# Wide conversion pieces, deferred transposing reads and the place of the value products in a top-k attention and MLP kernel

## The chip, the cores and the metric

The kernel runs on one core of one Trainium2 chip. The time is that of one execution on the device in microseconds (us), and a kernel is judged by the median of its runs. All inputs and the output lie in HBM.

## What is computed

An attention block that keeps the 32 largest scores of a row, and a two-layer MLP with a smooth activation:

```python
batch, n_heads, seq, head_dim = (8, 8, 576, 64)
scores = scale * np.matmul(q, k.transpose(0, 1, 3, 2))
kth = np.partition(scores, -top_k, axis=-1)[..., -top_k:-top_k + 1]
scores = np.where(scores >= kth, scores, -1000000000.0)
scores = scores - np.max(scores, axis=-1, keepdims=True)
attn = np.exp(scores)
attn = attn / (np.sum(attn, axis=-1, keepdims=True) + 1e-09)
x = np.matmul(attn, v)            # heads side by side: 4608 rows of 512
h = x @ w_in                      # 512 -> 2048
g = np.where(h >= 1, h, np.where(h <= -1, 0.0, (h + 1) ** 2 / 4))
out = g @ w_out                   # 2048 -> 512
```

`q`, `k` and `v` are float32. The two weight matrices are float64, so that the kernel reads 8 bytes per weight (16.8 MB in all) and makes float32 values of them itself.

## The kernel before

**Steps.** The unit of work is a step: 128 query rows of two heads against all 576 keys. There are 144 of them, 18 for each batch entry. Four steps with the same rows (all eight heads) make a chunk of 128 rows of `x`, and there are 36 chunks. The step runs over the engines like this:

- TensorE (PE) makes the scores `sp` (L351); ScalarE (ACT) copies them to `s` (L352).
- VectorE (DVE) finds the 32nd largest score of each row: pairwise maxima and minima `more` and `less` (L365), lists of eight (`max`, L413 to L439) with `match_replace` between them (L372), a scan that merges the lists (L444), and the masking of the exponentials `e` (L451). ACT makes `e` (L388).
- The weights of the step, `e` divided by its sum, have to be transposed. In the first steps PE does this by matmuls with a diagonal matrix `diag` (L401, L466) and ACT copies the result to `wT` (L469). In all later steps `move_w` does it: ACT splits `e` into 16-bit halves (`halves`, L481; one buffer), SP's queue writes them to HBM (`rows`, L483) and reads them back transposed (`wT`, L484; four buffers).
- `values` multiplies `wT` with the values (`po`, L498; L506 for the steps with the last rows of two batch entries), and ACT copies `po` to `xT` (L511). `po` uses the three PSUM buffers of the tag `ph`.

**The MLP.** When a chunk is complete, `mlp` puts its 32 pieces of work into the list `pending`: eight `hidden` (16 TensorE instructions `ph`, L531, with ACT's `r` and `g`, L535 and L542, and three of GpSimd (POOL), L547 to L549) and sixteen `final` (2 instructions `py`, L554, of 512 columns). `advance` takes them from the list between the parts of the steps, in amounts that a small model of the time in the kernel decides (`due`, `pe_time`, `usable`). One unit of `cost` is one 128-column product or a quarter of a `final`; a chunk has 128 units.

**The conversion of the weights.** In the first steps ("early") the float64 words are converted as well. A piece has 128 x 256 weights: its words are loaded by SP into one of eight slots of `room` (L132; the slots lie in the space of the second `kT` and `v_in`, and carry these names in the profile), ACT makes `units` from the low words and the sign of the high words (L145, L146), DVE shifts the high words (`bits`, L154), and POOL adds the two into `w_in` or `w_out` (L156). There are 64 pieces. Four are converted ahead of the first step, seven in each of the steps 0 to 7, four in step 8. Later, `inspect_piece` (L171) reads all weights a second time, 256 words at a time, to see that none is too small for the method.

**Keys, queries and values.** From the third batch entry on, `turn` transposes keys and queries as `move_w` does weights: ACT makes `parts` (L276), SP writes `lines` (L278) and reads them back transposed (L279). `turned_keys_of` does a fifth of a batch entry's keys in every second step, and issues the loads of the values (`v_in` L193, `v_tail` L196 and L200) in the last three of these parts.

**The order.** The instructions of PE, DVE, ACT and POOL stand in the order in which the program issues them (`manual_schedule`). The order of SP, which issues all DMAs, is made by the framework's scheduler. All of them are queues: an instruction that waits holds up those behind it.

Of the kernel before, what the change touches and what calls it, by code (L numbers as in the profile page):

```python
# [11 lines left out]
F32 = mybir.dt.float32  # L12
# [14 lines left out]
def kernel(  # L27
# [14 lines left out]
    P = 128  # L42
# [62 lines left out]

    WC = 256
    n_pieces = NK * DFF // WC + NF * DM // WC
    n_steps = B * (NT * NHP + NHP // 2)
    excess = const.tile([P, 2 * n_steps + n_pieces], F32, name="excess")
    signs = const.tile([P, 2, n_pieces], F32, name="signs")  # L110

# [13 lines left out]

    def load(pool, i, bufs=3):
        if i < n_pieces and i not in loaded:
            if room:
                loaded[i] = room[i % 8]
            else:  # L130
                loaded[i] = pool.tile([P, 2 * WC], U32, name="raw", bufs=bufs)
            nc.sync.dma_start(out=loaded[i], in_=pieces_of_weights[i][1].bitcast(U32))  # L132

    def words_of(pool, i, bufs=3):
        load(pool, i, bufs)
        words = loaded.pop(i).rearrange("p (n t) -> p n t", t=2)
        return words[:, :, 0], words[:, :, 1]

    def convert_piece(pool, i, any_size):

        lo, hi = words_of(pool, i)
        dst = pieces_of_weights[i][0]
        units = pool.tile([P, WC], F32, name="units", bufs=3)
        if not any_size:
            nc.scalar.activation(units, lo, AF.Identity, bias=one, scale=2.0 ** -52)  # L145
            nc.scalar.activation(units.bitcast(BF16).rearrange("p (n t) -> p n t", t=2)[:, :, 1], hi.bitcast(F32), AF.Sign)  # L146
        else:
            nc.scalar.activation(units, lo, AF.Identity, bias=two, scale=2.0 ** -51)
            sign = pool.tile([P, WC], F32, name="sign", bufs=3)
            nc.scalar.activation(sign, hi.bitcast(F32), AF.Sign)  # L150
        yield

        bits = pool.tile([P, WC], U32, name="bits", bufs=3)
        nc.vector.tensor_scalar(bits, hi, 3, None, ALU.logical_shift_left)  # L154
        if not any_size:
            nc.gpsimd.tensor_tensor(out=dst.bitcast(I32), in0=bits.bitcast(I32), in1=units.bitcast(I32), op=ALU.add)  # L156
        else:
            nc.gpsimd.tensor_tensor(out=bits.bitcast(I32), in0=bits.bitcast(I32), in1=units.bitcast(I32), op=ALU.add)
            size = pool.tile([P, WC], F32, name="units", bufs=3)
            nc.scalar.activation(size, hi.bitcast(F32), AF.Abs)  # L160
            nc.vector.scalar_tensor_tensor(out=sign, in0=size, scalar=TINY, in1=sign, op0=ALU.is_ge, op1=ALU.mult)

            nc.vector.tensor_scalar(bits.bitcast(F32), bits.bitcast(F32), LARGEST, -LARGEST, ALU.min, ALU.max)
            nc.gpsimd.tensor_tensor(out=dst, in0=sign, in1=bits.bitcast(F32), op=ALU.mult)
        yield

    def inspect_piece(pool, i):

        lo, hi = words_of(pool, i, 1)
        for x in range(2):  # L170
            nc.scalar.activation(lo.bitcast(F32), hi.bitcast(F32), AF.Sign, bias=tiny[:, x:x + 1],  # L171
                                 accum_out=signs[:, x, i:i + 1])


    def run(ctx, paired):
# [12 lines left out]
        def load_values(b):  # L188
            v_in = stage.tile([P, H, NT, D], F32, name="v_in")
            v_tl = v_tails[b % 2]  # L190
            yield v_in, v_tl
            for h in range(0, H, 2):
                nc.sync.dma_start(out=v_in[:, h:h + 2], in_=whole(v, b)[:, h:h + 2])  # L193
                yield
            for j in range(2):
                nc.sync.dma_start(out=v_tl[0][j * TL:(j + 1) * TL, j::2, :],  # L196
                                  in_=v[b, j::2, SM:S, :].rearrange("h p d -> p h d"))
            for hp in range(NHP):
                g = hp % 2
                nc.sync.dma_start(out=v_tl[1][g * TL:(g + 1) * TL, 2 * hp:2 * hp + 2, :],  # L200
                                  in_=v[b, 2 * hp:2 * hp + 2, SM:S, :].rearrange("h p d -> p h d"))
            yield

# [68 lines left out]
        def turn(x, dst):  # L272

            n = x.shape[0]
            parts = stage.tile([P, 2, H * D], U16, name="parts", tag="k_tl", bufs=1)[0:n]
            nc.scalar.copy(parts, x.rearrange("p h d -> p (h d)").bitcast(U16).rearrange("p (k t) -> p t k", t=2))  # L276
            lines = dram.tile([P, 2, H * D], U16, name="lines")[0:n]
            nc.sync.dma_start(out=lines, in_=parts)  # L278
            nc.sync.dma_start_transpose(dst.bitcast(U16), lines.rearrange("p t k -> (p t) k"))  # L279

        def turned_keys_of(b):
# [14 lines left out]

            blocks = {0: load_block(0)}
            yield got
            for c in range(NT + 1):
# [3 lines left out]
                turn(blocks.pop(c)[0:n], kT[:, :, c * P:c * P + n])  # L303
                if c == 1:
                    loads = load_values(b)
                    got["v"], got["v_tl"] = next(loads)
                if 1 <= c < NT:
                    next(loads)
                elif c == NT:
                    for _ in loads:  # L310
                        pass
                yield got
# [164 lines left out]
        def move_w(st):  # L477
# [4 lines left out]
            rows = dram.tile([P, 2, 2 * S], U16, name="rows")  # L482
            nc.sync.dma_start(out=rows, in_=halves)  # L483
            nc.sync.dma_start_transpose(wT.bitcast(U16), rows.rearrange("p t k -> (p t) k"))  # L484

# [116 lines left out]
        def convert(time):  # L602
# [8 lines left out]
            usable[converted] = time  # L611
            for i in range(begun, converted + (7 if room else 3)):
                load(words, i)

        def inspect():
            nonlocal inspected
            if paired and inspected < n_pieces:
                inspect_piece(late, inspected)
                inspected += 1


        K_TIME, PIECE_TIME, UNIT_TIME, SLOTS, EARLY_SHARE = 10.1, 0.55, 0.218, 7, 48
        pe_time, dve_time, done, scored, ready_at, usable = 9.0, 12.0, {}, {}, {}, {0: 0.0}

        def advance(amount, until):

            nonlocal spent, due, pe_time
            due = due + amount if pending else 0.0
            pe_time = max(pe_time, until - 4.0)
            while pending:  # L630
                cost, pieces, work, _ = pending[0]
                if pieces > converted or usable[pieces] > pe_time + 0.5:
                    break
                if due < cost or pe_time >= until:
                    break
                pending.popleft()
                due -= cost
                spent += cost
                pe_time += cost * UNIT_TIME
                work()  # L640
            due = min(due, 24.0)
# [12 lines left out]
        if paired:  # L654
            for x in (stage.tile([P, NHP, S], F32, name="kT").rearrange("p h n -> p (h n)"),
                      stage.tile([P, H, NT, D], F32, name="v_in").rearrange("p h c d -> p (h c d)")):
                room.extend(x[:, c:c + 2 * WC].bitcast(U32) for c in range(0, 8 * WC, 2 * WC))

# [6 lines left out]
        fetch(0)  # L665
        prep = None
        state = []
# [29 lines left out]
        next(first)  # L697
        for i in range(2, 8 if room else 3):
            load(words, i)
# [3 lines left out]
        begin_at(0)  # L703
        for i in range(3):
            convert(13.0)
        for _ in first_top(state[0]):
# [20 lines left out]
        for m in range(n + 2):  # L727
# [14 lines left out]
            if m < n:  # L742
                top_k = weights(state[m], state[m - 1] if m > 0 else None, state[m + 1] if m + 1 < n else None)
                parts = [1] * SLOTS if early else [1, 1, 0, 1, 1, 1, 1]
                start = max(dve_time, scored[m])
                now_converting = range(SLOTS)
                dve_time = start + K_TIME + PIECE_TIME * min(len(now_converting), n_pieces - converted)
                done[m] = dve_time
                state[m]["by_tensor"] = early or m >= n - 2
            for slot in range(SLOTS):  # L750
# [6 lines left out]
                elif slot == 3 and late is not None:  # L757
                    if m % 2:
                        inspect()
                    elif paired:  # L760
                        load(late, inspected, 1)
                if slot == 1 and 1 <= m <= n and state[m - 1]["by_tensor"]:
# [12 lines left out]
                if slot == 2 and not early:  # L775
                    values_until((m - 2) // 2 * 2)
                if slot == (4 if early else 2):
                    begin_at(m + 2)
                if slot == (6 if early else 1):
# [4 lines left out]
                    if prep is not None and (m % 2 == 0 or next_keys == 1):  # L784
# [59 lines left out]
```

## Time and profile before

| | |
|---|---|
| median of 3 runs | 1515.24 us (1515.05 to 1516.16) |
| profiled execution | 1516.81 us, span 1514.6 us, mean granted clock 0.98 |
| PE, DVE, ACT, POOL busy | 1441.9, 1412.7, 1167.1, 921.8 us |
| DMA | 259.76 MB, mean 172 GB/s |
| `units`, `bits`, add (L145, L146, L154, L156) | 64 instructions each |

In the profile, a row of a group reads: line, engine, operation, what is written from what, shapes, count | busy time, mean of one | idle time before, and what ended it. In a timeline a row begins with the start in us from the begin of the span and the duration in us; `[1.75 <-PE pw L466]` at its end means that the engine was idle for 1.75 us before it, until a `pw` of PE. PEld is the loading of weights on TensorE, PEclk the granted share of TensorE's clock, SPq the issue of a DMA by SP. A matmul in float32 appears as two instructions.

### The profile page before, as it was taken

How to read it: one execution, taken by the hardware profiler on the slowest of the kernel's cores; microseconds unless marked ns; L12 is line 12 of the kernel's file. 1: busy time of each engine (PE TensorE's matmuls, PEld its weight loads, DVE VectorE, ACT ScalarE, POOL GpSimd, SP SyncE). 2: the span in 40 equal slices, each digit the busy share in tenths (PEclk: the TensorE clock that was granted, in tenths of full speed). 3: DMA queues.
4: the chain of work that ended last, by engine and by line, in shares of the span. 5: the costliest groups of instructions: out<-in, count | busy, mean ns of one | idle time of the engine just before them, and what ended most of it. 6: DMA issues, size and time to landing. Idle time of an engine off the chain costs nothing.

```text
span 1514.6 us, 32180 instructions
## 1 busy us (share of the span) xinstructions
PE 1441.9 (95%) x10625; PEld 1042.8 (69%) x10625; DVE 1412.7 (93%) x4424; ACT 1167.1 (77%) x2288; POOL 921.8 (61%) x1339
## 2 busy tenths in 40 slices
PE   5588999999999999999999999899999999999998
PEld 4466677777777777677777777666677777777675
DVE  7888999999999999999999999999999999999912
ACT  7896878787778888787778888677777887777732
POOL 4563666666666666566666666566666666666630
PEclk7798999999999999999999999999999999999999
DMA  9542567775687777886677877786677777656510
GB/s 258 159 136 61 147 173 177 194 199 160 166 190 202 197 195 187 206 205 171 167 199 199 201 185 189 183 215 172 162 198 179 208 181 179 160 157 153 143 29 17
DMA packets 512448, 259.76 MB, mean 172 GB/s; under 512 B 459152, under 2 KB 467344, under 8 KB 512272
## 3 DMA queue, kind: packets, MB, share of 16 engines
q1 hardware_dynamic: 512272, 257.62, 65.6%
q8 instruction: 86, 1.41, 0.4%
q14 instruction: 90, 0.74, 0.2%
HBM read 62.91 MB, written 102.04 MB: 109 GB/s over the span
## 4 chain that ended last, share of the span: by engine, by line
PE 85%; ACT 8%; DMA 2%; issue 2%; POOL 1%; DVE 0%; SPq 0%; ACTq 0%; POOLq 0%; DVEq 0%
PE py L554 32%; PE ph L531 30%; PE sp L351 10%; PE po L498 10%; PE pw L466 2%; ACT halves L481 1%; ACT e L388 1%; ACT units L145 1%; PE po L506 1%; DMA rows<-halves 1%; ACT s L352 1%; DMA wT<-rows 1%; ACT wT L469 1%; ACT raw L171 0%; ACT g L542 0%
## 5 line engine op out<-in xcount | busy, mean ns | idle before, releaser
L531 PEld LDWEIGHTS ph<-xT,w_in 128*128 128x128 f32 x4608 | 547.0, 192 | 101.7 <-issue 82.2
L531 PE MATMUL ph<-xT,w_in 128*128 128x128 f32 x4608 | 557.2, 276 | 3.2 <-POOL w_in L156 3.1
L554 PE MATMUL py<-w_out,g 128*128 128x512 f32 x1152 | 551.0, 603 | 0.0
L547 POOL TENSOR_SCALAR r<-r 128x256 f32<-128x256 f32 x276 | 161.5, 585 | 447.2 <-ACT r L535 447.1
L372 DVE MATCH_REPLACE8 more<-tops,more 128x288 f32<-128x288 f32 x864 | 375.1, 437 | 0.0
L554 PEld LDWEIGHTS py<-w_out,g 128*128 128x128 f32 x1152 | 198.1, 191 | 181.2 <-issue 165.3
L481 ACT COPY halves<-e 128x1152 uint16<-128x1152 uint16 x266 | 291.9, 1143 | 15.5 <-DMA rows<-halves 14.5
L451 DVE SCALAR_TENSOR_TENSOR e<-s,kth,e 128x577 f32<-128x577 f32 x288 | 251.8, 909 | 3.6 <-ACT e L388 3.5
L549 POOL TENSOR_TENSOR g<-r,g 128x256 f32<-128x256 f32 x280 | 227.8, 814 | 22.0
L535 ACT ACTIVATE r<-ph,half 128x256 f32<-128x256 f32 (+1 forms) x296 | 136.1, 460 | 130.3 <-PE ph L531 104.2
L388 ACT ACTIVATE e<-s,nmax 128x576 f32<-128x576 f32 x288 | 222.4, 773 | 4.7
L404 POOL TENSOR_SCALAR e<-e,rz 128x576 f32<-128x576 f32 x266 | 223.4, 850 | 0.0
L352 ACT ACTIVATE s<-sp 128x576 f32<-128x576 f32 x288 | 172.0, 650 | 52.4 <-PE sp L351 51.9
L548 POOL TENSOR_TENSOR r<-r 128x256 f32<-128x256 f32 x276 | 191.3, 693 | 23.0
L351 PE MATMUL sp<-kT,qT 64*128 64x288 f32 x1024 | 162.9, 434 | 10.9 <-ACT kT L254 9.5
L498 PE MATMUL po<-wT,v_in 128*64 128x128 f32 x2048 | 143.4, 281 | 17.3 <-ACT g L542 15.3
L498 PEld LDWEIGHTS po<-wT,v_in 128*64 128x64 f32 x2048 | 117.0, 140 | 52.4 <-ACT g L542 40.1
L351 PEld LDWEIGHTS sp<-kT,qT 64*128 64x128 f32 x1024 | 89.4, 188 | 66.6 <-ACT r L535 25.0
L542 ACT ACTIVATE g<-ph,minus 128x256 f32<-128x256 f32 x280 | 130.1, 465 | 0.0
L413 DVE MAX8 tops<-more 128x8 f32<-128x288 f32 x288 | 125.4, 443 | 0.0
L365 DVE TENSOR_TENSOR less<-s 128x576 f32<-128x576 f32 x144 | 123.8, 860 | 0.0
L365 DVE TENSOR_TENSOR more<-s 128x576 f32<-128x576 f32 x144 | 109.9, 763 | 11.9 <-ACT s L352 11.9
(88 smaller groups left out, 1397.7 us busy)
## 6 DMA issues: line engine op xcount, KB each, us to landing
rows<-halves SPq DMA_DIRECT2D x133, 576.0 KB, 3.0
lines<-parts SPq DMA_DIRECT2D x48, 256.0 KB, 2.8
q_in<-in_q_dram SPq DMA_DIRECT2D x32, 256.0 KB, 4.0
kT<-in_moe_w_in_dram SPq DMA_DIRECT2D x32, 256.0 KB, 3.2
v_in<-in_moe_w_out_dram SPq DMA_DIRECT2D x32, 256.0 KB, 3.2
v_in<-in_v_dram SPq DMA_DIRECT2D x32, 256.0 KB, 4.2
raw<-in_moe_w_in_dram SPq DMA_DIRECT2D x32, 256.0 KB, 3.1
out_dram<-y SPq DMA_DIRECT2D x32, 256.0 KB, 3.2
```

The lines of the kernel that those rows point to most:

```text
L351: nc.tensor.matmul(*x, start=True, stop=True)
L365: nc.vector.tensor_tensor(out=x, in0=s[:, :, 0:SH], in1=s[:, :, SH:S], op=op)
L372: nc.vector.match_replace(out=st["rest"][:, i, :], in_to_replace=eight(st["tops"], i, r - 8), in_values=src[:, i, :], imm_value=LOWEST)
L388: nc.scalar.activation(e[:, i, :], s[:, i, :], AF.Exp, bias=nmax[:, i:i + 1])
L404: nc.gpsimd.tensor_scalar(st["e"][:, i, :], st["e"][:, i, :], rz[:, i:i + 1], 1.0, ALU.mult, ALU.mult)
L451: nc.vector.scalar_tensor_tensor(out=st["all"][1][:, i, :], in0=st["all"][0][:, i, :], scalar=last[i], in1=st["all"][1][:, i, :], op0=ALU. ...
L481: nc.scalar.copy(halves[:, :, i * S:(i + 1) * S], st["e"][:, i, :].bitcast(U16).rearrange("p (k t) -> p t k", t=2))
L498: nc.tensor.matmul(po[j * D:(j + 1) * D], v_in[:, h, c, :] if c < NT else v_tl[0][:, h, :], wT[:, block(j, c)], start=(c == 0), stop=(c == ...
L531: nc.tensor.matmul(ph[:, i], w_in[:, kk, f * P:(f + 1) * P], xT[:, kk], start=(kk == 0), stop=(kk == NK - 1))
L548: nc.gpsimd.tensor_tensor(out=r, in0=r, in1=r, op=ALU.mult)
L549: nc.gpsimd.tensor_tensor(out=g, in0=r, in1=g, op=ALU.add)
L554: nc.tensor.matmul(py[0], gs[f // group][:, f % group], w_out[:, f, :], start=(f == 0), stop=(f == NF - 1))
```

## The change

There are three parts.

1. Pieces of 512 columns: 32 pieces, four slots in `room`, two pieces ahead of the first step and one in every second of the seven slots of a step, so four a step. The second look at the weights stays at 256 words.
2. `turn` keeps its transposing read in a list, `turns`. The list is issued by `finish_turns`: in `move_w` between the write of `rows` and its transposing read, and at the end of slot 3. The loads of values are no longer part of the steps of the keys: each step in which no part of the keys is due issues one of seven parts.
3. In the late steps, before a pair of `values`, work is taken from `pending` as long as the last one taken was a `hidden`, so that a `final` stands in front of the pair.

```diff
-    WC = 256
+    WC = 512
...
-                loaded[i] = room[i % 8]
+                loaded[i] = room[i % len(room)]
...
             for j in range(2):
                 nc.sync.dma_start(out=v_tl[0][j * TL:(j + 1) * TL, j::2, :],
                                   in_=v[b, j::2, SM:S, :].rearrange("h p d -> p h d"))
+            yield
             for hp in range(NHP):
...
-            yield
+                if g:
+                    yield
...
-            nc.sync.dma_start_transpose(dst.bitcast(U16), lines.rearrange("p t k -> (p t) k"))
+            turns.append(partial(nc.sync.dma_start_transpose, dst.bitcast(U16), lines.rearrange("p t k -> (p t) k")))
+
+        turns = []
+
+        def finish_turns():
+            while turns:
+                turns.pop(0)()
...
             blocks = {0: load_block(0)}
+            got["loads"] = load_values(b)
+            got["v"], got["v_tl"] = next(got["loads"])
...
-                if c == 1:
-                    loads = load_values(b)
-                    got["v"], got["v_tl"] = next(loads)
-                if 1 <= c < NT:
-                    next(loads)
-                elif c == NT:
-                    for _ in loads:
-                        pass
...
             nc.sync.dma_start(out=rows, in_=halves)
+            finish_turns()
             nc.sync.dma_start_transpose(wT.bitcast(U16), rows.rearrange("p t k -> (p t) k"))
...
-            for i in range(begun, converted + (7 if room else 3)):
+            for i in range(begun, converted + (len(room) or 2)):
                 load(words, i)
...
-        K_TIME, PIECE_TIME, UNIT_TIME, SLOTS, EARLY_SHARE = 10.1, 0.55, 0.218, 7, 48
+        K_TIME, PIECE_TIME, UNIT_TIME, SLOTS, EARLY_SHARE = 10.1, 0.9, 0.218, 7, 48
...
+        taken = None
+
+        def take():
+
+            nonlocal spent, due, pe_time, taken
+            cost, pieces, work, _ = pending[0]
+            if pieces > converted or usable[pieces] > pe_time + 0.5:
+                return False
+            pending.popleft()
+            due -= cost
+            spent += cost
+            pe_time += cost * UNIT_TIME
+            work()
+            taken = work.func
+            return True
...
-        for i in range(3):
-            convert(13.0)
+        convert(13.0)
...
-                now_converting = range(SLOTS)
+                now_converting = range(0, SLOTS, 2)
...
+                if slot == 3:
+                    finish_turns()
...
                 if slot == 2 and not early:
+                    if m % 2 == 0:
+                        while pending and taken is not None and taken.__name__ == "hidden" and take():
+                            pass
                     values_until((m - 2) // 2 * 2)
...
+                            value_loads = got.get("loads", value_loads)
+                    elif value_loads is not None:
+                        next(value_loads, None)
```

More of the change, by code (lines that the diff above doesn't have):

```diff
@@ L102 @@
             nc.gpsimd.memset(x[:, i * SPLIT:i * SPLIT + 1], LARGEST)
-    WC = 256
+    WC = 512
     n_pieces = NK * DFF // WC + NF * DM // WC
     n_steps = B * (NT * NHP + NHP // 2)
-    excess = const.tile([P, 2 * n_steps + n_pieces], F32, name="excess")
-    signs = const.tile([P, 2, n_pieces], F32, name="signs")
+    excess = const.tile([P, 2 * n_steps + 2 * n_pieces], F32, name="excess")
+    signs = const.tile([P, 2, 2 * n_pieces], F32, name="signs")
     pieces_of_weights = []
@@ L124, with load, words_of @@
     loaded, room = {}, []
-    def load(pool, i, bufs=3):
-        if i < n_pieces and i not in loaded:
+    def load(pool, i, bufs=3, parts=1):
+        if i < n_pieces * parts and i not in loaded:
             if room:
-                loaded[i] = room[i % 8]
+                loaded[i] = room[i % len(room)]
             else:
[L131 to L135, printed above, removed]
+                loaded[i] = pool.tile([P, 2 * WC // parts], U32, name="raw", bufs=min(bufs, 2))
+            c = i % parts * (WC // parts)
+            nc.sync.dma_start(out=loaded[i], in_=pieces_of_weights[i // parts][1][:, c:c + WC // parts].bitcast(U32))
+    def words_of(pool, i, bufs=3, parts=1):
+        load(pool, i, bufs, parts)
         words = loaded.pop(i).rearrange("p (n t) -> p n t", t=2)
@@ L142, in convert_piece @@
         dst = pieces_of_weights[i][0]
-        units = pool.tile([P, WC], F32, name="units", bufs=3)
+        units = pool.tile([P, WC], F32, name="units", bufs=2 if any_size else 3)
         if not any_size:
@@ L148, in convert_piece @@
             nc.scalar.activation(units, lo, AF.Identity, bias=two, scale=2.0 ** -51)
-            sign = pool.tile([P, WC], F32, name="sign", bufs=3)
+            sign = pool.tile([P, WC], F32, name="sign", bufs=1)
             nc.scalar.activation(sign, hi.bitcast(F32), AF.Sign)
         yield
-        bits = pool.tile([P, WC], U32, name="bits", bufs=3)
+        bits = pool.tile([P, WC], U32, name="bits", bufs=1 if any_size else 3)
         nc.vector.tensor_scalar(bits, hi, 3, None, ALU.logical_shift_left)
@@ L158, in convert_piece @@
             nc.gpsimd.tensor_tensor(out=bits.bitcast(I32), in0=bits.bitcast(I32), in1=units.bitcast(I32), op=ALU.add)
-            size = pool.tile([P, WC], F32, name="units", bufs=3)
+            size = pool.tile([P, WC], F32, name="units", bufs=2)
             nc.scalar.activation(size, hi.bitcast(F32), AF.Abs)
@@ L167, in inspect_piece @@
     def inspect_piece(pool, i):
-        lo, hi = words_of(pool, i, 1)
+        lo, hi = words_of(pool, i, 1, 2)
         for x in range(2):
@@ L616, in inspect @@
             nonlocal inspected
-            if paired and inspected < n_pieces:
+            if paired and inspected < 2 * n_pieces:
                 inspect_piece(late, inspected)
                 inspected += 1
-        K_TIME, PIECE_TIME, UNIT_TIME, SLOTS, EARLY_SHARE = 10.1, 0.55, 0.218, 7, 48
+        K_TIME, PIECE_TIME, UNIT_TIME, SLOTS, EARLY_SHARE = 10.1, 0.9, 0.218, 7, 48
         pe_time, dve_time, done, scored, ready_at, usable = 9.0, 12.0, {}, {}, {}, {0: 0.0}
+        taken = None
[11 more added lines that the diff above has]
+            return True
         def advance(amount, until):
-            nonlocal spent, due, pe_time
+            nonlocal due, pe_time
             due = due + amount if pending else 0.0
             pe_time = max(pe_time, until - 4.0)
[L630 to L640, printed above, removed]
+            while pending and due >= pending[0][0] and pe_time < until and take():
+                pass
             due = min(due, 24.0)
@@ L656, in run @@
                       stage.tile([P, H, NT, D], F32, name="v_in").rearrange("p h c d -> p (h c d)")):
-                room.extend(x[:, c:c + 2 * WC].bitcast(U32) for c in range(0, 8 * WC, 2 * WC))
+                room.extend(x[:, c:c + 2 * WC].bitcast(U32) for c in range(0, 4 * WC, 2 * WC))
             warm = ps.tile([P, NT, P], F32, name="warm", tag="a", bufs=2)
@@ L665, in run @@
         fetch(0)
-        prep = None
+        prep, value_loads = None, None
         state = []
@@ L697, in run @@
         next(first)
-        for i in range(2, 8 if room else 3):
+        for i in range(2, len(room) or 2):
             load(words, i)
@@ L760, in run @@
                     elif paired:
-                        load(late, inspected, 1)
+                        load(late, inspected, 1, 2)
                 if slot == 1 and 1 <= m <= n and state[m - 1]["by_tensor"]:
@@ L775, in run @@
                 if slot == 2 and not early:
+                    if m % 2 == 0:
+                        while pending and taken is not None and taken.__name__ == "hidden" and take():
+                            pass
                     values_until((m - 2) // 2 * 2)
```

## The prediction

> **What bounds the kernel now.** I first read the page: busy shares and slices.
>
> ```profile
> PE 1441.9 (95%) x10625; PEld 1042.8 (69%) x10625; DVE 1412.7 (93%) x4424; ACT 1167.1 (77%) x2288; POOL 921.8 (61%) x1339
> ...
> PE   5588999999999999999999999899999999999998
> ...
> PEclk7798999999999999999999999999999999999999
> ```
>
> TensorE is the long engine, but not in the first four slices (150 us): there it idles and its clock is cut. So there are two stages, and each is read by itself. The early stage, by stretches of 15 us:
>
> ```profile
> core 0: us, PE busy (x) PEld busy (x) DVE busy (x) ACT busy (x) POOL busy (x), PEclk, DMA share, GB/s
> ...
> 30.00:45.00 15.00, 7.98 (x52) 6.15 (x52) 14.29 (x46) 12.95 (x32) 7.67 (x9) 0.73 0.76 225
> 45.00:60.00 15.00, 9.63 (x58) 8.09 (x59) 12.48 (x41) 12.75 (x31) 8.53 (x12) 0.73 0.53 166
> 60.00:75.00 15.00, 9.83 (x62) 7.88 (x60) 13.57 (x46) 11.55 (x27) 7.68 (x10) 0.77 0.52 158
> 75.00:90.00 15.00, 14.88 (x129) 13.25 (x128) 9.61 (x30) 14.40 (x37) 9.56 (x16) 1.00 0.32 97
> ```
>
> DVE and ACT are both near full; DMA is not after 30 us. The timeline shows which leads. All DVE idle between 45 and 60 us (2.5 us) is `bits` (L154) waiting for POOL's add (L156), and that add waits for ACT's `units`. ACT is what is late. Its own step, on its timeline:
>
> ```profile
> 44.62 0.69 ACT L401 ACTIVATE diag<-ident,rz 128x128 f32<-128x128 f32 x2
> 45.22 0.51 ACT L145 ACTIVATE units<-kT,one 128x256 f32<-128x256 uint32 x1
> 45.76 0.49 ACT L146 ACTIVATE units<-kT 128x256 bf16<-128x256 f32 x1
> ...
> 48.89 1.07 ACT L469 COPY wT<-pw 128x512 f32<-128x512 f32 x2 [1.75 <-PE pw L466]
> ...
> 61.56 1.07 ACT L469 COPY wT<-pw 128x512 f32<-128x512 f32 x2 [1.74 <-PE pw L466]
> ```
>
> From `wT` to `wT` is one step, 12.67 us. Start to start a piece takes 0.54 us (L145) + 0.36 (L146) = 0.90, seven make 6.3 us; 1.74 us is a wait for the `pw` matmuls, which take 3.78 us at clock 0.50; other ACT work is 4.6 us.
>
> From 300 us on a tile (four steps) takes 38.15 us. DVE shows no idle, but its instructions with two SBUF inputs are stretched (`less` 1.28 us at 409.14, else 0.75). PE starts every matmul at its shortest pitch (112 ns for `ph`, 429 for `py`), so PE sets the pace and can gain only where it stands. Between 150 and 1440 us its gaps of 0.5 us and more add up to 20 us: about 2.1 at 165 to 182 us (keys' transposes), 0.6 for `wT<-rows`, 2.1 at the end, and 15.3 in front of `values`, all after `ph` and all released by `ACT g L542`: 0.76 (206 us), 2.52 (286), 2.56 (633), 5.87 (985) and four of 0.89 (1026 to 1144). Two of them, and a normal entry between:
>
> ```profile
> 975.81 3.96 PE L531 MATMUL ph<-xT,w_in 128*128 128x128 f32 x34
> 985.63 1.98 PE L498 MATMUL po<-wT,v_in 128*64 128x128 f32 x16 [5.87 <-ACT g L542]
> ...
> 1026.19 1.09 PE L498 MATMUL po<-wT,v_in 128*64 128x128 f32 x16 [0.89 <-ACT g L542]
> ```
>
> The group behind 5.87 us takes 1.98 instead of 1.09 us, as the clock was cut. `po` shares three PSUM buffers with `ph`, so it waits until ACT has emptied an older `ph`. Why ACT was late, by SP's and ACT's timelines:
>
> ```profile
> 971.73 1.25 SPq L279 DMA_TRANSPOSE kT<-lines  x1
> 973.03 0.63 SPq L291 DMA_DIRECT2D k_block<-in_k_dram  x1
> 973.71 0.61 SPq L294 DMA_DIRECT2D k_block<-in_k_dram  x1
> 974.36 3.34 SPq L200 DMA_DIRECT2D v_tail<-in_v_dram  x5
> 977.80 0.55 SPq L483 DMA_DIRECT2D rows<-halves  x1
> ...
> 981.98 2.20 ACT L481 COPY halves<-e 128x1152 uint16<-128x1152 uint16 x2 [4.86 <-DMA rows<-halves]
> ```
>
> `halves` was ready at 971.4, its write was issued at 977.8 behind eight other issues, and ACT waited 4.86 us for the one `halves` buffer.
>
> **The change, part by part.** The base is the profiled execution: 1516.8 us (span 1514.6 and 2.2 around it), 1.6 above the median of 1515.24.
>
> 1. *Wide pieces.* 64 pieces of 256 become 32 of 512; per step four instead of seven; all are done in step 7 instead of step 8. ACT has no row of 512 strided words. Its slope from copies: `parts` (1024) 935 ns and `halves` (1152) 1040 ns start to start, 105 ns over 128 elements, 0.82 ns each; 256 more cost 0.21 us, so a wide piece takes 0.75 + 0.57 = 1.32 instead of 1.80 us, and 32 save 15 us of ACT. [...]
>  Steps 0 to 3: ACT falls from 6.3 to 5.3 us, but only one piece is left between `diag` and `wT`, so the wait for `pw` grows by about 0.47: -0.5 each, -2.1. Step 4 (18.1 us, with a burst of five `ph` pairs): -0.5. Step 5: no wait for `pw` (clock 1.0), -1.0. Step 6: -0.3, since DVE then binds: 9.14 us for a step without conversions, its shortest from 300 us on, plus 4 x 0.33 for `bits` plus collisions, near 11. Step 7 has two pieces instead of seven: 12.9 to 10.4, -2.5. Step 8 has none instead of four: 11.8 to 10.0, -1.8. Step 9 no longer has `pw`: -1.7. Sum -9.9.
>  At nothing: DVE `bits` (7 x 0.20 us against 4 x 0.33). POOL: an add takes 0.68 us for 256; 2-element adds of L407 take 0.15, so 512 take about 1.2: 4.9 a step against 4.8, and POOL idles half of the stage. SP: 32 issues fewer. The first loads double (0.5 MB more ahead of the second keys, 1.7 us at 297 GB/s), but these keys are copied by ACT only at 15.6 us, behind the exponentials: 0, at most +1. Room stays 2 MB, four slots for eight; a slot is loaded again three conversions ahead of its use, some 6 us against 3.2 to land.
>  [...] `less` loses 0.54 us, `bits` takes 0.80 instead of 0.28. [...] Beside 2 us of DVE idle a step I count 0, and +4 for the range.
>
> 2. *Values behind a final.* In the order as built, the 24 `ph` ahead of every other pair of values get one `py` matmul behind them; it is taken from after the values, so no work is added. `ph` to `po` costs 205 ns against 112 and `py` to `po` 523 against 430: 93 ns either way, no gain from the order itself. The gain is cover: 0.86 us of matmul while ACT empties `ph`. That takes away the 0.76 and four 0.89 (-4.3), and 0.86 from each of 2.52, 2.56 and 5.87 (-2.6). From 1182 us on the old order happened to have `py` there, and the gap is 0.03. Price: the next scores come 0.86 us later; DVE starts `more` 2.3 to 3.6 us after the scores' copy is done, so 0.
>
> 3. *Transposing reads behind rows' writes, value loads in steps of their own.* SP is ordered by the framework, not by hand, so I compared SP's order as built. It hardly moves: between the keys' read and the rows' write that was late at 977.8 there are six issues instead of seven (-0.6 us); at the one late at 626 there are eight instead of six (+1.2); at the first batch boundary it is the same. In six steps the read of keys now stands behind the rows it used to precede, but there PE does not stand. Worth: -0.6 + 1.2, about +0.5 on PE with the cover above. Bounds: -16 if all gaps before `values` go, with some 4 us of half clock; +5 if each of three boundaries loses 1.5.
>
> The last 150 rows of PE's order are the same in both, and at step 13 both have done the same 236 units of the hidden layer's queue, so an early gain is neither lost nor grown there; the tail of 74 us behind the last selection stays.
>
> Sum: -9.9 - 4.3 - 2.6 + 0.5 = -16.3, giving 1500.5 for the profiled base and 1499 as a median.
>
> **Rivals.**
> - *Boundaries clear altogether* (SP's smaller shifts are enough that ACT never waits for `halves`): -9.9 - 16 - 5 of clock, 1484. For it: 4.86 us of ACT's wait hang on eight issues. Against: the list is nearly the same. 0.14.
> - *The second and third part do nothing*: the order of SP is not what the edit says, and the gaps move to other places with the phase. Only -10 or less of part 1: 1505 to 1510. 0.16.
> - *Slower: scores come too late.* In 1016 to 1165 us a tile took 39.1 instead of 38.15 us; `more` there had 0.03 us of slack in the pair's step. If the final ahead of the scores puts every tile into that rhythm, 26 more tiles pay 0.95: +25 against -10 and -3, 1527. It decides once slack at the pair's step falls by more than 2.3 us; the final takes 0.86, so 1.4 more would be needed, say from ACT's copy of the scores behind a late `g`. 0.10.
>
> **How the numbers follow.** 0.60 for the forecast, alone 1490 to 1506. The range 1481 to 1514 takes in the first two rivals and leaves out the slower one and the far ends. This kernel's runs lie within 0.1%; 0.2% is 3 us. Faster 0.84 (forecast, clear boundaries and most of the second rival), same 0.06, slower 0.10.
>
> **What would show it.** L145 and L146 fall from 64 to 32 each, at 0.7 us in the mean, 15 us less ACT; the step's period before 75 us falls to about 12.1; `pw` is gone from 115 us on; the `po` gaps of 0.89 are gone; gaps near 620 and 960 us remain, smaller than 6 us. Wrong: steps of 12.6 us with ACT waiting longer for `pw` (clock), or tiles of 39 us in the middle, or no `po` gap at all.

## The result, and the profile after

The changed kernel takes 1508.58 us (median of 17 runs, 1503.05 to 1513.81), the kernel before 1514.04 on the same chip (17 runs, 1509.95 to 1517.54). The ratio is 0.9967, with an interval of 0.9956 to 0.9979: 5 us faster, where 16 were forecast. The direction and the range held, the size did not. The profiled execution took 1507.81 us with a span of 1506.0; the profiled one of before lay 2.8 above the median of these runs, that of the changed kernel 0.8 below its own, so that the two spans differ by 8.6 us, more than the medians.

The page of the changed kernel, busy shares and slices:

```profile
PE 1441.7 (96%) x10605; PEld 1034.8 (69%) x10605; DVE 1411.9 (94%) x4392; ACT 1158.4 (77%) x2221; POOL 908.5 (60%) x1309
...
PE   5698899999999999999999999999999999999998
...
PEclk6799899999999999999999999999999999999999
```

The busy time of PE is what it was; the fifth slice (151 to 188 us) shows PE at 8 and its clock at 8 tenths, where both stood at 9 before. So PE lost less time before 150 us, but found a new hole just behind. The stretches around it, engine by engine:

```profile
core 0: us, PE busy (x) PEld busy (x) DVE busy (x) ACT busy (x) POOL busy (x), PEclk, DMA share, GB/s
...
120.00:135.00 15.00, 12.96 (x90) 7.77 (x87) 12.73 (x46) 8.13 (x19) 1.74 (x4) 1.00 0.27 77
135.00:150.00 15.00, 12.60 (x91) 11.09 (x90) 15.00 (x48) 11.79 (x24) 4.44 (x5) 0.89 0.32 92
150.00:165.00 15.00, 10.36 (x42) 5.97 (x41) 11.49 (x40) 10.59 (x20) 10.38 (x17) 0.68 0.50 132
```

From 120 to 135 us POOL does almost nothing (1.74 us): no `hidden` reaches it. From 150 to 165 us PE issues only 42 matmuls in 15 us and DVE stands for 3.5 us. This is where the early gain went, as the experiments show.

ACT's step in the early stage, on the timeline (the same excerpt as in the prediction):

```profile
45.40 0.75 ACT L146 ACTIVATE units<-v_in,one 128x512 f32<-128x512 uint32 x1
46.18 0.78 ACT L147 ACTIVATE units<-v_in 128x512 bf16<-128x512 f32 x1
49.07 1.07 ACT L472 COPY wT<-pw 128x512 f32<-128x512 f32 x2 [2.11 <-PE pw L469]
...
61.52 1.07 ACT L472 COPY wT<-pw 128x512 f32<-128x512 f32 x2 [2.12 <-PE pw L469]
```

The step is 12.45 us instead of 12.67. A wide piece starts its second half 0.78 us after its first, and the next instruction stands 0.65 us behind that: 1.43 us. The wait for `pw` has grown by 0.38 us.

PE's waits in front of `values`, at the late batch boundary and in the four tiles behind it:

```profile
977.81 1.02 PE L558 MATMUL py<-w_out,g 128*128 128x512 f32 x2
981.91 1.33 PE L502 MATMUL po<-wT,v_in 128*64 128x128 f32 x10 [3.08 <-ACT g L546]
...
1020.51 1.02 PE L558 MATMUL py<-w_out,g 128*128 128x512 f32 x2
1021.57 1.09 PE L502 MATMUL po<-wT,v_in 128*64 128x128 f32 x16
```

A `final` (`py`) now stands ahead of `po`. The wait of 5.87 us has become 3.08, and the four waits of 0.89 us are gone; which part did this is asked below.

### The profile page after: what moved, and what is told of

Its sections match the earlier page's. It is cut to its first block, busy times and chain, and to the rows that moved or that the text cites. A ratio compares the mean times of both kernels' runs of the same rounds, so it can differ in the third digit from the quotient of the medians.

```text
span 1506.0 us, 31908 instructions
## 1 busy us (share of the span) xinstructions
PE 1441.7 (96%) x10605; PEld 1034.8 (69%) x10605; DVE 1411.9 (94%) x4392; ACT 1158.4 (77%) x2221; POOL 908.5 (60%) x1309
## 2 busy tenths in 40 slices
DMA packets 510318, 260.93 MB, mean 173 GB/s; under 512 B 460992, under 2 KB 469184, under 8 KB 510144
## 4 chain that ended last, share of the span: by engine, by line
PE 66%; DVE 20%; ACT 6%; DMA 3%; issue 3%; POOL 1%; SPq 1%; ACTq 0%; POOLq 0%
PE ph L535 24%; PE py L558 24%; PE sp L354 8%; PE po L502 8%; DVE more L375 5%; DVE e L454 4%; DVE less L368 2%; DVE more L368 2%; DMA rows<-halves 2%; PE pw L469 2%; DVE tops L416 2%; DVE tops L424 2%; DVE tops L435 2%; DVE seconds L442 2%; DVE tops L388 1%
## 5 line engine op out<-in xcount | busy, mean ns | idle before, releaser
L551 POOL TENSOR_SCALAR r<-r 128x256 f32<-128x256 f32 x276 | 146.8, 532 | 453.6 <-ACT r L539 453.4
L484 ACT COPY halves<-e 128x1152 uint16<-128x1152 uint16 x268 | 293.6, 1143 | 13.4 <-DMA rows<-halves 13.4
L454 DVE SCALAR_TENSOR_TENSOR e<-s,kth,e 128x577 f32<-128x577 f32 x288 | 259.6, 937 | 0.8 <-ACT e L391 0.6
L553 POOL TENSOR_TENSOR g<-r,g 128x256 f32<-128x256 f32 x280 | 240.9, 860 | 22.0
L407 POOL TENSOR_SCALAR e<-e,rz 128x576 f32<-128x576 f32 x268 | 223.4, 843 | 12.6 <-DVE rz L400 12.6
```

The lines of the kernel that those rows point to most:

```text
L407: nc.gpsimd.tensor_scalar(st["e"][:, i, :], st["e"][:, i, :], rz[:, i:i + 1], 1.0, ALU.mult, ALU.mult)
L454: nc.vector.scalar_tensor_tensor(out=st["all"][1][:, i, :], in0=st["all"][0][:, i, :], scalar=last[i], in1=st["all"][1][:, i, :], op0=ALU. ...
L484: nc.scalar.copy(halves[:, :, i * S:(i + 1) * S], st["e"][:, i, :].bitcast(U16).rearrange("p (k t) -> p t k", t=2))
L553: nc.gpsimd.tensor_tensor(out=g, in0=r, in1=g, op=ALU.add)
```

## Where the time is, stage by stage

The scan of DVE (L447 after, L444 before) occurs once in each step; its start marks the steps. The table sums the profiled executions (us): from the scan of step 0 to that of step 12, from there to the scan of step 143, and what lies outside (start and tail).

| kernel | steps 0 to 12 | steps 12 to 143 | outside | span |
|---|---|---|---|---|
| before | 148.1 | 1267.2 | 99.3 | 1514.6 |
| changed | 144.9 | 1261.6 | 99.5 | 1506.0 |
| part 1 alone (e1) | 142.7 | 1262.7 | 99.6 | 1505.0 |
| part 2 alone (e2) | 145.0 | 1265.4 | 100.0 | 1510.4 |
| part 3 alone (e3) | 149.2 | 1270.2 | 99.8 | 1519.2 |
| share 28, changed (e4) | 137.9 | 1257.8 | 101.1 | 1496.8 |
| share 28, before (e8) | 144.3 | 1265.9 | 99.6 | 1509.8 |
| last value rows loaded from GpSimd's queue (e10) | 146.1 | 1250.1 | 101.3 | 1497.5 |
| share 28 and e10's loads (e12) | 137.9 | 1253.2 | 96.9 | 1487.9 |

A row is one execution, and a profiled execution lay between 3.2 us below (e1) and 5.3 above (e3) the median of its kernel. The changed kernel and three others told of below with the same early steps (e5, e7, e10) gave 144.9, 144.8, 144.5 and 146.1 in the first column. The kernel before, e2 and e3, which have the same first ten steps, gave 148.1, 145.0 and 149.2. So differences under 2 us, and with narrow pieces under 4, mean little there.

## The experiments

**Each part alone.** Three kernels take one part of the change each, on the kernel before.

```diff
e1:
-    WC = 256
+    WC = 512
...
-                now_converting = range(SLOTS)
+                now_converting = range(0, SLOTS, 2)
e2:
+                    if m % 2 == 0:
+                        while pending and taken is not None and taken.__name__ == "hidden" and take():
+                            pass
                     values_until((m - 2) // 2 * 2)
e3:
-            nc.sync.dma_start_transpose(dst.bitcast(U16), lines.rearrange("p t k -> (p t) k"))
+            turns.append(partial(nc.sync.dma_start_transpose, dst.bitcast(U16), lines.rearrange("p t k -> (p t) k")))
...
+            got["loads"] = load_values(b)
+            got["v"], got["v_tl"] = next(got["loads"])
```

> Part 1 alone (wide pieces, four a step); values and SP's issues as before. Theory A (the early gain was spent again in steps 7 to 11, because the list of MLP work runs empty in step 7 and comes back as a burst): step 12 is reached 2 to 3 us earlier than before, as in the full change, and the stall of 3 to 4 us near step 10 is there; the gaps of 0.9 us and the long one before the values remain as before, so the whole is 0 to 4 us faster. Theory B (part 1 keeps its 10 us and parts 2 and 3 cost time early): 8 us or more faster, step 12 reached 8 us earlier.

> Part 2 alone (a final in front of each pair of values). By the sum on record: the four gaps of 0.89 and the one of 0.76 us are gone, the long ones shrink by 0.86 each, 6 to 7 us faster at most; early steps unchanged within 1 us. Rival: the gaps only move (to DVE waiting for scores, or to other places) and the time is the same within 2 us.

> Part 3 alone (deferred transposing reads, value loads in steps of their own). By the sum on record: 0, between -1 and +3 us, since SP's order as built hardly changes; the long gaps near 630 and 980 us stay. Rival: 5 us or more faster, the long gaps gone.

Measured: e1 1510.08 us, ratio 0.9973 (0.9960 to 0.9987); e2 1510.41, 0.9968 (0.9953 to 0.9983); e3 1515.99, 1.0004 (0.9990 to 1.0017). The first two alone are worth 4 and 5 us, together 5 and not 9. In part they remove the same thing: with wide pieces the amounts that `advance` takes shift, a `py` then stands ahead of the pairs by itself, and the four waits of 0.89 us are gone in e1 too, which I had not expected. The stall near step 10, expected in e1, was not there either: its step 10 took 9.97 us, and its twelve steps 142.7. In e2 the long waits did not shrink as expected: those of 0.5 us and more at the three boundaries add up to 12.5 us, against 11.6 before. Part 3 by itself does nothing that is measured.

**The early list.** One constant of the changed kernel is lowered: the units per step that `advance` may take while weights are still converted.

```diff
-        K_TIME, PIECE_TIME, UNIT_TIME, SLOTS, EARLY_SHARE = 10.1, 0.9, 0.218, 7, 48
+        K_TIME, PIECE_TIME, UNIT_TIME, SLOTS, EARLY_SHARE = 10.1, 0.9, 0.218, 7, 28
```

> The full change with EARLY_SHARE 28 in place of 48, so that each early step takes 24 to 32 units of MLP work and 28 units are left for step 8. Theory A: PE no longer idles in steps 8 and 9, the stall of DVE near 153 us (3.5 us) is gone or below 1 us, step 12 is reached 3 to 7 us earlier than in the full change, and the whole is 3 to 7 us faster than it (1502 to 1505). Theory C (the shortfall lies in the wide pieces themselves, 1.43 us instead of 1.32, and in the wait for pw): step 12 within 1.5 us of the full change, and no gain.

Measured: 1497.72 us, ratio 0.9880 (0.9854 to 0.9905). That is 11 us below the changed kernel, more than theory A asked for. The first twelve steps take 137.9 us instead of 144.9. From step 12 to 143 it is 3.8 less, though PE's waits there are not shorter in sum (10.0 us in e4, 8.0 in the changed kernel, counting those of 0.5 us and more); that part is left open. By the program's own count, the units taken after steps 4 to 9 are 32, 64, 96, 128, 128, 144 in the changed kernel, with nothing left in `pending` after step 7; with a share of 28 they are 16, 48, 76, 100, 112, 136, and the list never runs empty. In e4's stretches the hole is gone, with 105 matmuls where the changed kernel had 42:

```profile
core 0: us, PE busy (x) PEld busy (x) DVE busy (x) ACT busy (x) POOL busy (x), PEclk, DMA share, GB/s
...
150.00:165.00 15.00, 14.56 (x105) 9.57 (x106) 15.00 (x46) 13.22 (x27) 12.43 (x17) 1.00 0.71 193
```

What happens when the list has run empty is read from the changed kernel's timelines, of PE first, then ACT, then DVE:

```profile
136.83 0.76 PE L354 MATMUL sp<-kT,qT 64*128 64x288 f32 x4 [1.38 <-ACT qT L330]
...
138.82 6.98 PE L535 MATMUL ph<-xT,w_in 128*128 128x128 f32 x48
...
146.07 1.95 PE L535 MATMUL ph<-xT,w_in 128*128 128x128 f32 x16
148.74 2.05 PE L535 MATMUL ph<-xT,w_in 128*128 128x128 f32 x16 [0.71 <-ACT g L546]
150.62 1.02 PE L558 MATMUL py<-w_out,g 128*128 128x512 f32 x2
151.58 1.24 PE L354 MATMUL sp<-kT,qT 64*128 64x288 f32 x8
156.27 1.11 PE L253 MATMUL pk<-ident,k_in 128*128 128x128 f32 x4 [3.45 <-ACT s L355]
```

```profile
154.84 0.47 ACT L539 ACTIVATE r<-ph,half 128x256 f32<-128x256 f32 x1 [2.64 <-POOL g L553]
155.21 0.47 ACT L546 ACTIVATE g<-ph,minus 128x256 f32<-128x256 f32 x1
155.57 1.19 ACT L355 ACTIVATE s<-sp 128x576 f32<-128x576 f32 x2
```

```profile
156.79 0.86 DVE L368 TENSOR_TENSOR more<-s 128x576 f32<-128x576 f32 x1 [3.51 <-ACT s L355]
```

With nothing in the list, PE stands between its short pieces of other work (1.38 us is one of five such waits from 125 to 138 us). Its granted clock, 1.00 from 120 to 135 us, is 0.89 from 135 to 150, and 0.50 in the two single microseconds from 139 to 141. There the next chunk comes at once as three `hidden`, 48 matmuls in 6.98 us, where 48 take 5.52 at a clock of 1.00 (e10, at 622.68 us; 1.00 from 615 to 630). Two more `hidden` and a `final` follow before the next scores (`sp`, 151.58 us). The results of the `hidden` queue at POOL, whose chain `r`, `r`, `g` has the steps' own `e` in it (L407). ACT waits 2.64 us for it with the copy of the next scores, `s`, behind, and PE and DVE both wait some 3.5 us for `s`. Step 10 takes 13.4 us, against 9.62 before.

The empty list alone does not do this. In e1 it runs empty in the same way, with the same counts up to step 9. Up to step 12 the order of DVE is the same as in the changed kernel, and that of PE differs in one place: in e1 the scores stand ahead of the last two `hidden` and the `final`:

```profile
139.28 6.29 PE L539 MATMUL ph<-xT,w_in 128*128 128x128 f32 x48
...
145.93 0.76 PE L358 MATMUL sp<-kT,qT 64*128 64x288 f32 x4
150.28 0.76 PE L358 MATMUL sp<-kT,qT 64*128 64x288 f32 x4 [3.59 <-ACT kT L255]
150.97 5.44 PE L539 MATMUL ph<-xT,w_in 128*128 128x128 f32 x32
156.24 1.02 PE L562 MATMUL py<-w_out,g 128*128 128x512 f32 x2
```

PE stands here too, but DVE does not, and step 10 takes 9.97 us. What put the scores behind in the changed kernel is its own part 2: in step 10 the list begins with `hidden` only, no `final` of an older chunk being left to stand between them, and the rule that takes work until a `final` stands in front takes two `hidden` and a `final`. In the four kernels with this order step 10 took 13.4, 13.4, 12.6 and 13.4 us (changed, e5, e7, e10); with part 2 and a list that is not empty (e4) it took 10.0.

**The same constant on the kernel before.** Is it the smaller share that gains, whatever the pieces?

```diff
-        K_TIME, PIECE_TIME, UNIT_TIME, SLOTS, EARLY_SHARE = 10.1, 0.55, 0.218, 7, 48
+        K_TIME, PIECE_TIME, UNIT_TIME, SLOTS, EARLY_SHARE = 10.1, 0.55, 0.218, 7, 28
```

> The kernel before with nothing but the early share at 28 instead of 48. Theory A (the wide pieces save early time, and the list of hidden units that runs empty takes it back): with the narrow pieces the steps are longer and the list is not what limits, so the share brings little, 0 to 4 us less than before, 1511 to 1515, and step 12 scans no earlier than 170 us. Rival S: the burst of hidden units in steps 4 and 5 is what costs, whatever the pieces: the share alone brings the 11 us that it brought on the changed kernel, 1503 to 1505, with step 12 near 166 us.

Measured: 1512.09 us, ratio 1.0003 (0.9990 to 1.0016), step 12 at 170.0. In the first twelve steps narrow pieces take 145.0 to 149.2 us at a share of 48 (before, e2, e3) and 144.3 at 28; wide ones 142.7 to 146.1 at 48 (changed, e1, e5, e7, e10) and 137.9 to 138.1 at 28 (e4, e6, e12). In the means each alone is worth some 3 us, no more than the scatter, and both together 9. The pieces are worth more where the list feeds PE: 6.4 us at a share of 28 (144.3 to 137.9).

**Empty list or burst?** A share of 28 does two things: it keeps the list filled, and it halves what is taken at once in step 4. Two kernels separate them.

```diff
e13:
-                advance((EARLY_SHARE if early else share) / SLOTS if m < n else 32.0, now)
+                advance(((48 if m < 5 else 16) if early else share) / SLOTS if m < n else 32.0, now)
e14:
+                advance(((28 if m < 6 else 48) if early else share) / SLOTS if m < n else 32.0, now)
```

> The changed kernel with the early share of 48 kept in step 4 and lowered to 16 from step 5 on: step 4 has its burst of 32 units as before, but the list never runs empty (32, 48, 64, 80, 96, 124 units taken after steps 4 to 9, against 32, 64, 96, 128, 128, 144 in the changed kernel). A share of 28 throughout took the twelve first steps from 144.6 to 138.0 us; two things in it could have done so. If it is the list that runs empty in step 7: nearly all of the 6.6 us, twelve steps in 138 to 140 us, 1497 to 1500 in all. If it is the burst of step 4 that holds up the scores: 143 to 146 us, 1506 to 1510.

> The opposite: 28 in steps 4 and 5, 48 from step 6 on, so that step 4 takes 16 units, and the list still runs nearly empty in step 7 and empty in step 8 (16, 48, 88, 120, 128, 144 units taken after steps 4 to 9). If the empty list costs the time: twelve steps in 143 to 146 us, 1506 to 1510. If the burst of step 4 does: 138 to 140 us, 1497 to 1500.

Measured: e13 took 139.3 us for the twelve steps, although its burst remained (17.71 us for step 5, 17.57 in the changed kernel); e14 took 141.9, between its two theories, with the hole back (PE clock 0.66 from 150 to 165 us). So keeping the list filled alone brings 5.5 of the 7.0 us between the changed kernel and e4, and a smaller burst alone 3.0; the two overlap. In e14 two `hidden` and a `final` stand ahead of the scores as in the changed kernel, and PE waited 3.20 us for `s` although its clock had been 1.00 from 135 to 150 us. But DVE waited only 0.52 and step 10 took 10.3 us: how much of PE's wait reaches DVE depends on more than this order, and whether the lower clock added to it is not shown. The totals went another way: e13 1506.56 us, ratio 0.9946 (0.9922 to 0.9970), where 1497 to 1500 was expected, and e14 1514.13, 1.0002 (0.9989 to 1.0014), slower than either theory had it. The early gain of e13 was there at step 12 and was given back at the batch boundaries: PE's waits at the three boundaries are 3.66, 4.36 and 2.95 us, against 1.66, 3.25 and 3.08 in the changed kernel. In e14 PE waits at 616 us for the transposing read of queries:

```profile
616.22 1.37 PE L354 MATMUL sp<-kT,qT 64*128 64x288 f32 x8 [3.14 <-DMA qT<-lines]
```

SP wrote those `lines` at 609.69 us and issued their read at 612.28. Six more waits for `qT<-lines` lie between 573 and 1049 us. Why the queries come that late in this order is not settled.

**What holds the boundaries.** At the boundary near 628 us in the changed kernel ACT waits 3.10 us for the one buffer of `halves`, with the copies that PE needs behind. First: a second buffer.

```diff
-        xtp = ctx.enter_context(tc.tile_pool(name="xtp", bufs=5))
+        xtp = ctx.enter_context(tc.tile_pool(name="xtp", bufs=3))
...
-            halves = late.tile([P, 2, 2 * S], U16, name="halves")
+            halves = late.tile([P, 2, 2 * S], U16, name="halves", bufs=2)
```

> The changed kernel with two buffers for `halves` instead of one (and three for the group's xT instead of five, to make room). What is asked is what makes the two waits of some 3.1 us that stay near 628 and 978 us, where py waits for po and po for ScalarE's copy of the last finals. Theory H: ScalarE's pieces for `halves` wait for the rows' write of the step before to let go of the one buffer, and the finals' copies stand behind them in ScalarE's order; then both waits shrink to under 1 us and the time is 3 to 6 us below the changed kernel, near 1503 to 1505. Rival P: the copies are late because of their own place in the order; then the two gaps stay within 0.5 us of 3.1 and the time stays within 2 us of 1508.6. The early part is not touched: the scan of step 12 is expected at 170 us by both.

> Both edits in one: a share of 28 instead of 48 in the early steps, and two buffers for `halves`. By theory H something is left in the spread version too (one wait for ScalarE near 273 us, 2.9 us, and about 1 us each at 645 and 990 for transposed rows): 1494 to 1496. By rival P the second buffer adds nothing to the spread version: 1497 to 1499.

Measured: e5 1510.16 us, ratio 0.9982 (0.9973 to 0.9992), no better than the changed kernel; e6 1495.54, 0.9896 (0.9878 to 0.9914), by its ratio the same as e4, although its time lies where theory H had it. Both edits also take `xT` from five buffers to three, and what that costs is not told apart. ACT's wait did go, but PE's moved, a few matmuls on, to the transposed rows:

```profile
634.05 1.98 PE L502 MATMUL po<-wT,v_in 128*64 128x128 f32 x16 [2.82 <-DMA wT<-rows]
```

So the buffer was a symptom, and the theory that it is the cause falls: the rows themselves come late. SP's timeline in the changed kernel shows why; the `halves` that this write sends were ready at 618.82 us:

```profile
618.32 1.25 SPq L288 DMA_TRANSPOSE kT<-lines  x1
619.62 1.49 SPq L303 DMA_DIRECT2D k_block<-in_k_dram  x1
621.16 0.60 SPq L194 DMA_DIRECT2D v_in<-in_v_dram  x1
621.82 4.02 SPq L202 DMA_DIRECT2D v_tail<-in_v_dram  x6
625.92 0.54 SPq L486 DMA_DIRECT2D rows<-halves  x1
628.95 2.40 SPq L488 DMA_TRANSPOSE wT<-rows  x1
```

Six small loads of the last value rows, 0.67 us of issue each, stand ahead of the one write that PE is waiting for. Second, therefore: these loads left out from the third batch entry on (e7; the rows they would bring stay stale), and then the same loads issued from POOL's queue (e10; nothing is left out).

```diff
e7:
-            for j in range(2):
+            for j in range(2 if b < 2 else 0):
...
+                if b < 2: nc.sync.dma_start(out=v_tl[1][g * TL:(g + 1) * TL, 2 * hp:2 * hp + 2, :],
e10:
-                nc.sync.dma_start(out=v_tl[0][j * TL:(j + 1) * TL, j::2, :],
+                (nc.sync if b < 2 else nc.gpsimd).dma_start(out=v_tl[0][j * TL:(j + 1) * TL, j::2, :],
...
-                nc.sync.dma_start(out=v_tl[1][g * TL:(g + 1) * TL, 2 * hp:2 * hp + 2, :],
+                (nc.sync if b < 2 else nc.gpsimd).dma_start(out=v_tl[1][g * TL:(g + 1) * TL, 2 * hp:2 * hp + 2, :],
```

> The changed kernel without the reloading of the last value rows for the batches from the third on, so that these rows are stale there: some DMA issues of SP fall away at each group's start. Theory Q (part 3's subject): the SP queue's issues ahead of the rows' writes at the groups' starts hold the writes up; then the gaps at the boundaries shrink and the time falls by 2 to 5 us, to 1504 to 1506. Rival: these issues are done long before anything needs SP; then 1508.6 within 1.5 us, as with part 3 alone, which gave 0.0 us.

> The changed kernel with the loads of the last value rows (from the third batch on) issued by GpSimd instead of SP; nothing is left out, and PE, VectorE and ScalarE have the same instructions in the same order. Leaving these 36 issues of 0.6 us out gave 1497.6. Theory Q (they stand ahead of the rows' writes in SP's queue at the groups' starts, and the finals then wait): as good as without them, 1497 to 1500, with the PE gaps near 280, 628 and 978 us below 0.7 us each. Rival (GpSimd pays for the issues[...], and its chain r, g stands behind them, or what helped was the traffic that fell away and not the queue): 1504 to 1510.

Measured: e7 1497.63 us, ratio 0.9901 (0.9885 to 0.9918), more than its theory asked for; e10 1497.47, 0.9886 (0.9867 to 0.9905), as good as without the loads. SP and PE at the same boundary in e10:

```profile
617.67 0.63 SPq L300 DMA_DIRECT2D k_block<-in_k_dram  x1
618.35 0.61 SPq L303 DMA_DIRECT2D k_block<-in_k_dram  x1
619.00 1.63 SPq L486 DMA_DIRECT2D rows<-halves  x1
```

```profile
628.03 1.02 PE L558 MATMUL py<-w_out,g 128*128 128x512 f32 x2
629.09 1.09 PE L502 MATMUL po<-wT,v_in 128*64 128x128 f32 x16
```

The write goes out 0.5 us after its `halves` were ready (618.47 us) instead of 7.1, and there is no wait before `po`. The same bytes are moved (260.93 MB in both profiles), so it was not the traffic. What is gone from SP's queue ahead of the write is the issue of six loads, 4.02 us. PE, DVE and ACT have the same instructions in the same order as in the changed kernel. One caution: POOL's order is written by hand, so the loads also go out at another moment (for instance at 565 us instead of 622), and the rest of SP's order shifts with them (a load of `v_in` from 621 us to 609). Queue and moment are not told apart.

The size comes out of the rows. From step 12 to 143 e10 needs 11.6 us less. The three boundary waits add up to 1.66 + 3.25 + 3.08 = 8.0. Behind the two long ones the granted clock was lower as well. In the changed kernel it is 0.89 in each of the stretches 630 to 645 and 970 to 985 us, and 0.50 in the single microseconds from 634 to 636 and from 982 to 984; in e10 it is 1.00 from 615 to 645 and from 965 to 995. The lost 0.11 of 15 us is, as an estimate, 1.65 us of work each. Together 11.3, closer than single executions can tell.

**Both.** The share of 28 and the loads from POOL in one kernel.

> The same with an early share of 28 instead of 48. The share alone gave 1497.7 (ratio 0.988), and there the gaps near 280 and 978 had gone or shrunk already. If the two savings are different time (the early 7 us from theory A, the boundaries' from Q): 1489 to 1493. If the share's 11 us had been mostly the boundaries in another phase: 1495 to 1498.

Measured: 1488.82 us (1488.01 to 1489.76), ratio 0.9826 (0.9808 to 0.9845). That is 27 us under the kernel before in the same comparison and some 20 under the changed one. In the spans it is 18.1 us below the changed kernel, where the share alone is 9.2 and the loads alone 8.5; in the medians the two are worth 11 each and 20 together. So they are for the most part different time, and this version beats both kernels.

## Why the prediction was right or wrong

1. *Early, -9.9: this term failed.* Measured -3.2 from step 0 to 12, no more than the scatter of the stage. Its pieces: steps 0 to 3, forecast -2.1, were -2.3. Steps 4 and 5, forecast -1.5, were 0.1 longer: the burst of `hidden` remained and came one step later. Steps 6 to 11, forecast -6.3, were -1.1.

   Two sentences of the prediction failed together. The first is that both orders have done the same 236 units at step 13, so that an early gain is neither lost nor grown. The count is right, but it is one of the end of the stretch and not within it: in step 7, where I booked the largest single gain (-2.5), the list ran empty. The second is the price of part 2, "the next scores come 0.86 us later", put at 0. In step 10 it was not one `final` but two `hidden` and a `final`, and that step took 3.8 us more than before; e1, with the same empty list and without part 2, does not have this stand. So the rival of scores that come too late happened, once, in the early stage and not in every tile.

   The size of the pieces themselves was too large as well. With the list kept filled (e4) the twelve steps are 10.2 us shorter than before, but 3.8 of these are the share's own (e8), so that the pieces are worth some 6.4 us and not 9.9, as far as single executions of this stage can tell.

2. *Sizes in the early stage.* A wide piece was put at 1.32 us and takes 1.43, so ACT saves 64 x 0.90 - 32 x 1.43 = 12 us and not 15: the slope of 0.82 ns, taken from 16-bit copies, was too flat for these instructions. All of ACT's busy time fell by 8.7 us, that of the pieces by 15. The wait for `pw` grew by 0.38 instead of 0.47, an add on POOL takes 1.33 to 1.36 us instead of 1.2, the step period came to 12.45 instead of 12.1, and the last `pw` of the stage started at 127 us, not before 115. What these adds cost DVE was put at 0, with +4 in the range, an estimate of mine; no run separates it. The longest `bits` took 0.81 us before and 1.20 in the changed kernel, against medians of 0.28 and 0.42; what stretched them is not shown.

3. *A `final` ahead of the values, -4.3 and -2.6: right for the short waits, not for the long ones.* The wait of 0.76 and the four of 0.89 are gone, in e2 as well. The boundaries' waits went from 2.52, 2.56 and 5.87 to 1.66 (now for `y`), 3.25 and 3.08 us, in sum -3.0, but not by the cover: part 2 alone (e2) does not shorten their sum, and part 1 alone (e1) already brings the longest to 3.13. Steps 12 to 143 fell by 5.6 in the profiles, with -6.4 forecast for both late parts; as this pair of executions overstated the whole by 3.5 us, and the long waits went for another reason, that agreement is in part luck. What was also not seen: wide pieces alone remove the same 0.89 waits, so that the part's own share on top of part 1 is about 1 us at most (ratios 0.9973 and 0.9967).

4. *Transposing reads and value loads, +0.5: right, for the reason given.* SP's order hardly moves, and e3 measured 0.0. But the prediction's own excerpt of SP had five `v_tail` issues of 3.34 us ahead of the late write, and stopped at counting six issues for seven. The 11 us that lay there came when the loads left SP's queue (e10), and not when they were put into another step of the program (e3).

5. *The rivals.* "Second and third part do nothing" had the right time (1505 to 1510) and the wrong reason. Tiles of 39 us did not come: 38.2 us in the steady stage. The boundaries cleared altogether only with the loads off SP's queue, and then at 1497 and not at 1484 us, in the main as the early gain was not there (-2.0 in e10 for -9.9).

6. *Scatter.* Runs of one kernel were said to lie within 0.1%; 17 runs of either kernel spread by 0.5 and 0.7%. A single profiled pair overstated this change by 3.5 us.

## What to carry to other kernels

When a stage is shortened, follow the work that hides its waits step by step and not only to its end: a list that runs empty in the middle comes back as a burst. When a rule takes "work until", look at what it takes where the list looks different from the steady stage: here it took three pieces where one was meant. When a wait names an engine, follow it upstream through the queues until something is found that was ready and not sent; a second buffer in between only moves the wait. Small DMA issues had a price of their own here, 0.6 us of queue each, so keep them out of the queue that carries the transfer the critical engine waits for.

## What was not expected of the hardware

- An issue from POOL's queue took 0.60 to 0.66 us for the 32 KB loads, no more than SP's 0.60 to 0.68, and all 36 loads of e10 (of 32 and 64 KB) cost nothing that is measured: without them (e7) the time is the same.
- Around the end of a stand of some 3 us on TensorE the granted clock went down in the changed kernel: it was 1.00 from 630 to 633 us, 0.50 from 634 to 636 and 1.00 again from 637 (the stand of 3.25 us ended at 632.67). The length of the stand does not decide it alone: in the kernel before one of 2.56 us (until 633.56) had a clock of 0.89 from 630 to 645 us, and one of 2.52 us (until 286.44) had 1.00 from 270 to 300.
- The first twelve steps took from 144.5 to 146.1 us in four executions of the same instructions there, 148.1 and 149.2 in two of the kernel before's, and 137.9 to 138.1 in three once the stand of step 10 was gone.
